# Eight-head projections, spread by DMA, and a re-timed feed-forward in a fused attention and SwiGLU kernel

## The chip, the core and the metric

The kernel runs on one core of one Trainium2 chip. The metric is the device time in microseconds (us) of one execution, as the median of several runs. A core has five engines that work side by side and wait for each other through semaphores: TensorE (PE, matmuls into PSUM, its weight loads shown as PEld), VectorE (DVE), ScalarE (ACT), GpSimd (POOL) and SyncE (SP), which here issues every DMA, in order, on one queue.

## What is computed

```python
def reference(A_x, A_wqkv, A_wo, B_x, B_w1, B_w3, B_w2):
    x = A_x                                   # [1, 2048, 512], bf16
    xn = _layernorm(x, axis=-1)
    return x + _A_ref(xn, A_wqkv, A_wo) + _B_ref(xn, B_w1, B_w3, B_w2)

# _A_ref: 32 heads of 16 columns
qkv = (x @ wqkv).reshape(B, S, 3, H, Dh).transpose(2, 0, 3, 1, 4)
scores = einsum("bhqd,bhkd->bhqk", q, k) * (Dh ** -0.5)
o = einsum("bhqk,bhkd->bhqd", softmax(scores), v)
out = o.transpose(0, 2, 1, 3).reshape(B, S, D) @ wo

# _B_ref: F = 1792
h = silu(x @ w1) * (x @ w3)
out = h @ w2
```

`B_x` is not read: both branches take the normalised `A_x`.

## The kernel before

**A planner writes the order.** The Python code does not loop over the chip's work directly. It holds queues of candidate steps (score blocks, exps, copies, matmul tiles, DMAs) with an estimated cost for each, repeatedly emits the one that could start first, and records every dependence as a semaphore wait. So each engine receives a fixed list of instructions, whose order follows from the cost estimates, and a change of one step can move all the others.

**Groups and units.** The 32 heads form 8 groups of 4, since one head has 16 columns and a group's four heads sit in four 32-row bands of the array. The 2048 query rows form 4 quarters of 512. A quarter and a group make a query group, 32 in all, worked in order. Each is cut into units of 256 query rows (the first into 128, 128, 256, the last into 256, 128, 128): 66 units.

**Two passes over the scores.** For every unit the scores are made twice. Pass 1 (`p1_cand`, matmuls at line 799) writes two heads' scores of 128 queries by 512 keys into two PSUM banks, and VectorE reduces them to a row maximum (line 821): 1024 reduces of 1024 columns. There are 16 of them in a unit of 256 queries; the count up to now is what the planner calls a step (`p1_n`). After a unit's last reduce its negated maximum (line 862) is split into two bf16 parts by GpSimd (lines 838 and 840), transposed by a DMA (line 859) and put by two DMAs (line 855) into rows 16 and 17 of each head's band of `QT`. Pass 2 (`p2_cand`, line 935) makes the scores again, transposed, with these two rows adding minus the maximum, and ScalarE's exp (line 948) writes the probabilities into a slot of `PT` (44 slots of 512 columns, the first 16 of which hold x during the layer norm). A unit of 256 queries takes 32 exps, one of 128 takes 16. For the first two and the last three units (`FAST_AUG`) the two rows come from a matmul instead (`tile_QT2`), which projects the unit's queries again and adds the shift.

**After the exps.** `tile_PV` multiplies the probabilities with `Vaug`, the values with a column of ones; it may begin when at most 4 of the unit's exps are left (`PV_LEFT`), and gives its `PT` slots back as it goes. The sums of the exps are inverted and spread by a chain of transfers and GpSimd operations (lines 1031 to 1057, one unit at a time), except in the last three units (`FAST_PV`), where a second set of matmuls with ones and VectorE's reciprocal (line 1001) and product (line 1003) do it.

**Projections.** A key tile (`tile_KT`) is one group's keys for 512 rows: 16 matmuls and a copy by ScalarE (line 560) that adds a one to rows 16 and 17 through `kbias`. A query tile (`tile_QT`) is the same for a query group (copy at line 603). Their weights are kept in a padded form, 32 columns for a head, 16 of them zero. `QT` has three slots; slot ug % 3 can be written again when pass 2 has issued all matmuls of query group ug - 3.

**Feed-forward.** 14 blocks of 128 columns for each quarter, 56 steps. Each is a gate and an up tile of 16 matmuls, three ScalarE copies (lines 665, 667, 671) and three GpSimd operations (lines 650 to 654) into `hT`, which holds one quarter. `ffn_from` gives the step of pass 1 from which each may start. `tile_OUT` adds x, the feed-forward product and the projected attention of 128 rows; in the last quarter `tile_OUTA` does all but the attention and `tile_OUTB` the rest.

**Order of the column tiles.** `choose` hands out one tile at a time while pass 1 runs: a projection with a due step less than 8 ahead first, then PV, a projection less than 20 ahead, outputs, feed-forward, a projection less than 80 ahead. `fill_cand` adds matmuls without use where TensorE's load is low.

Of the kernel before, what the change touches and what calls it, by code (L numbers as in the profile page):

```python
# [5 lines left out]
FP32 = mybir.dt.float32  # L6
# [229 lines left out]
def _build(nc, A_x, A_wqkv, A_wo, B_w1, B_w3, B_w2, out):  # L236
# [12 lines left out]
    NPT = 44  # L249
# [8 lines left out]
    LAG = 44  # L258
# [7 lines left out]
    for qc in range(NQC):  # L266
        for g in range(NG):
            last = qc == NQC - 1 and g == NG - 1
            first = qc == 0 and g == 0
            for (q0, nq) in ([(0, 256), (256, 128), (384, 128)] if last else  # L270
                             [(0, 128), (128, 128), (256, 256)] if first else [(0, 256), (256, 256)]):
                units.append((qc, g, q0, nq))
    NU = len(units)
    FAST_AUG = {0, 1, NU - 3, NU - 2, NU - 1}
    FAST_PV = {NU - 3, NU - 2, NU - 1}
# [7 lines left out]
    with ctx:  # L283
        PT = sb("PT", [128, NPT, 512], BF16)
        x_sb = PT[:, 0:NT, :]
        xr = sb("xr", [128, 4, D], BF16)
# [10 lines left out]
        hT = sb("hT", [128, FC, 512], BF16)  # L297
        stg = {"wk": 0, "wv": DC, "wq": 2 * DC}
        STG_KEYS = {w: [("hT", i) for i in range(o, o + DC)] for w, o in stg.items()}
        wkst, wv, wqst = (hT[:, stg[w]:stg[w] + DC, :] for w in ("wk", "wv", "wq"))  # L300
        kbias = sb("kbias", [128, 1], FP32)
        wq = sb("wq", [128, DC * NG * 4, 32], BF16)
        wk_on = sb("wk_on", [128, DC * NG * 128], BF16)
        on_b = sb("on_b", [128, NG, 512], BF16)
        wk = wk_on[:, :].rearrange("p (a b) -> p a b", b=32)
# [23 lines left out]
        maskrow = sb("maskrow", [1, 128], BF16)  # L329
        onesrow = sb("onesrow", [1, 2], BF16)  # L330
# [21 lines left out]
        def qt_keys(qs, q0, nq, what):  # L352
            return [(what, qs, q) for q in range(q0 // 128, (q0 + nq) // 128)]

# [23 lines left out]
        def c_small(e):  # L378
            e.memset(maskrow[:, :], 0.0)
            e.memset(onesrow[:, :], 1.0)  # L380
            e.memset(mhalf[:, :], -0.5)
            e.memset(mone[:, :], -1.0)
            return e.memset(Z[:, :, :, :], 0.0)
        P.op("pool", c_small, writes=[("maskrow",), ("onesrow",), ("mhalf",), ("mone",), ("Z", 0), ("Z", 1)], occ=1.2)
        P.op("pool", lambda e: e.memset(maskrow[0:1, :].rearrange("p (j d) -> p j d", d=32)[:, :, 16:18], 1.0),
             writes=[("maskrow",)], occ=0.1)
        P.op("dve", lambda e: e.memset(wk[:, :, 16:32], 0.0), writes=[("wkpad",)] + ON0_KEYS, occ=0.95)
        P.op("dve", lambda e: e.memset(wq[:, :, 16:32], 0.0), writes=[("wqpad",)], occ=0.95)
# [3 lines left out]
        P.op("pe", lambda e: e.matmul(bank(4)[:, 0:1], maskrow[0:1, :], onesrow[0:1, 0:1], start=True, stop=True),  # L392
             reads=[("maskrow",), ("onesrow",)], writes=[("ps", 4)], occ=0.05, lat=0.3)
# [13 lines left out]
        def load_w(dst, w, off):  # L407
            P.dma(lambda e: e.dma_start(dst, wqkv_v[:, :, off * D:(off + 1) * D]), writes=STG_KEYS[w], lat=5.0)
        load_x(0)
        load_x(1)  # L410
        load_w(wkst, "wk", 1)
        load_w(wqst, "wq", 0)
        load_x(2)
        load_x(3)
        load_w(wv, "wv", 2)
# [10 lines left out]
        def pad_first(dst, src):  # L426
            return lambda e: e.tensor_scalar(
                dst.rearrange("p (c h) d -> p c h d", c=DC)[:, :, 0:4, 0:16],
                src[:, :, 0:64].rearrange("p c (h d) -> p c h d", d=16), 1.0, 0.0, ALU.mult, ALU.add)

        def pad_rest(dst, src, c):
            return lambda e: e.tensor_scalar(
                dst[:, c * NG * 4 + 4:(c + 1) * NG * 4, 0:16],
                src[:, c, 64:D].rearrange("p (a d) -> p a d", d=16), 1.0, 0.0, ALU.mult, ALU.add)

        def pad_first_a(dst, src):
            return lambda e: e.activation(
                dst.rearrange("p (c h) d -> p c h d", c=DC)[:, :, 0:4, 0:16],
                src[:, :, 0:64].rearrange("p c (h d) -> p c h d", d=16), ACTF.Identity)

        def pad_rest_a(dst, src, c):
            return lambda e: e.activation(
                dst[:, c * NG * 4 + 4:(c + 1) * NG * 4, 0:16],
                src[:, c, 64:D].rearrange("p (a d) -> p a d", d=16), ACTF.Identity)
        wq_all = wq[:, :, :]
        poolq["pad"].append(_Item(pad_first(wk, wkst), STG_KEYS["wk"], [("wk", 0)], 0.4))
        miscq.append(_Item(pad_first_a(wq_all, wqst), STG_KEYS["wq"], [("wq", 0)], 0.3))
        for c in range(DC):
            poolq["pad"].append(_Item(pad_rest(wk, wkst, c), STG_KEYS["wk"], [("wk", 1 + c)], 0.62,
                                      pred=lambda: ("KT", 0, NQC - 1) in done))  # L450
        WK_KEYS = [("wkpad",)] + [("wk", i) for i in range(DC + 1)] + ON0_KEYS
        WQ_KEYS = [("wqpad",)] + [("wq", i) for i in range(DC + 1)]
        wq4 = wq[:, :, :].rearrange("p (c g j) d -> p c g (j d)", c=DC, g=NG)
        wk4 = wk.rearrange("p (c g j) d -> p c g (j d)", c=DC, g=NG)
        poolq["pad"].append(_Item(lambda e: e.memset(Vaug[:, :, :, 16:17], 1.0), [],
                                  [("Vone",)], 2.4, pred=lambda: ("AUG", 0) in done))
        poolq["pad"].append(_Item(lambda e: e.memset(wo[:, :, :], 0.0), [], [("wo",)], 3.5,
# [62 lines left out]
        def tr_ready(t):  # L520
            done.add(("xn", t))
            pt_free.append(t)
            head_tiles.append(tile_tr(t))
            if t % XG == XG - 1:
                gi = t // XG
                head_tiles.append(tile_KT(0, gi))
                if gi == 0:
                    head_tiles.append(tile_QT(0))
# [22 lines left out]
        def tile_KT(g, sc, need=None):  # L551
            groups = []
            for c in range(DC):
                groups.append((lambda bk, c=c: col_groups(
                    bk, lambda i: wk4[:, c, g, 32 * i:32 * i + 32], lambda i: xnT[:, c, sc * 512:(sc + 1) * 512], 512,
                    start=c == 0, stop=c == DC - 1),
                    (WK_KEYS if g else [("wkpad",), ("wk", 0)]) + xnT_keys(sc * 512, 512), _c_mm(512), None))

            def evac(bk):
                return [_Item(lambda e: e.activation(KT[:, g, sc * 512:(sc + 1) * 512], bank(bk), ACTF.Identity,  # L560
                                                     bias=kbias[:, 0:1]),
                              [("ps", bk), ("kbias",)], [("KT", g, sc)], 0.57, 0.68,
                              cb=lambda op: done.add(("KT", g, sc)), name="first")]
            return _Tile("KT%d_%d" % (g, sc), groups, evac, need=need,
                         pred=lambda: all(("xnT", t) in done for t in range(sc * 4, sc * 4 + 4))
                         and (g == 0 or not poolq["pad"] or not _wk_pending()))

        def _wk_pending():
            return any(it.writes and it.writes[0][0] == "wk" for it in poolq["pad"])

        def tile_V(t, need=None):
            groups = []
            for c in range(DC):
                groups.append((lambda bk, c=c: col_groups(
                    bk, lambda i: xnT[:, c, t * 128 + 32 * i:t * 128 + 32 * i + 32], lambda i: wv[:, c, :], D,
                    start=c == 0, stop=c == DC - 1), STG_KEYS["wv"] + [("xnT", t)], _c_mm(512), None))
# [11 lines left out]
        def qt_groups(qc, g, q0, nq, stop_last):  # L588
            groups = []
            for c in range(DC):  # L590
                groups.append((lambda bk, c=c: col_groups(
                    bk, lambda i: wq4[:, c, g, 32 * i:32 * i + 32],
                    lambda i: xnT[:, c, qc * 512 + q0:qc * 512 + q0 + nq], nq,
                    start=c == 0, stop=stop_last and c == DC - 1, skip=not stop_last),
                    (WQ_KEYS if g or qc else [("wqpad",), ("wq", 0)]) + xnT_keys(qc * 512 + q0, nq), _c_mm(nq), None))
            return groups

        def tile_QT(ug, need=None):
            qc, g = divmod(ug, NG)
            qs = ug % 3  # L600

            def evac(bk):
                return [_Item(lambda e: e.activation(QT[:, qs, :], bank(bk), ACTF.Identity),  # L603
                              [("ps", bk)], qt_keys(qs, 0, 512, "QT"), _c_act(512),
                              cb=lambda op: done.add(("QT", ug)))]
            return _Tile("QT%d" % ug, qt_groups(qc, g, 0, 512, True), evac, need=need,
                         pred=lambda: (ug < 3 or p2_units_done[0] > ug_last[ug - 3])
                         and all(("xnT", t) in done for t in range(qc * 4, qc * 4 + 4))
                         and (ug == 0 or not _wq_pending()))

        def _wq_pending():
            return any(it.writes and it.writes[0][0] == "wq" for it in miscq)

        def tile_QT2(u):
# [10 lines left out]
            def evac(bk):  # L625
                return [_Item(lambda e: e.activation(QT[:, qs, q0:q0 + nq], bank(bk)[:, 0:nq], ACTF.Identity),
                              [("ps", bk)], qt_keys(qs, q0, nq, "QT"), _c_act(nq), cb=lambda op: done.add(("AUG", u)))]
# [5 lines left out]
        def ffn_from(sc, fc):  # L633
            last = sc == NQC - 1
            lo = sc * CHUNK + (100 if sc else 40)
            hi = (sc + 1) * CHUNK + (-48 if last else LAG)
# [801 lines left out]
```

## Time and profile before

| | us |
|---|---|
| median of 3 runs (1233.07 to 1240.68) | 1234.11 |
| the profiled execution | 1235.43 |
| its span, first to last instruction | 1233.4 |
| mean granted TensorE clock | 0.998 |

| group of instructions | count | busy us |
|---|---|---|
| pass 2 scores, matmul, L935 | 4224 | 568.3 |
| pass 1 scores, matmul, L799 | 2048 | 441.9 |
| key copies, ACT, L560 | 32 | 23.2 |
| query copies, ACT, L603 | 32 | 20.3 |
| gate and up copies, ACT, L665, L667, L671 | 168 | 105.6 |
| filler and x, matmul, `xnT` by `ident` | 1412 | 111.7 |

The profile gives the busy time of each engine, the chain of work that ended last, groups of instructions by line, a timeline, and busy times in chosen windows. In a group's line the columns are line, engine, operation, output and input tiles, count, then busy time, mean ns of one, and the idle time ahead of them with what ended it. Instructions of one engine overlap a little, so the mean of one can be longer than its share of the busy time. In a row of windows with all engines the order is PE, PEld, DVE, ACT and POOL, each with its number of instructions, then the granted TensorE clock, the DMA share and GB/s; a row for one line has the one engine.

### The profile page before, as it was taken

What the parts mean: (1) busy time and instruction counts of PE and PEld (TensorE: products, weight loads), DVE (VectorE), ACT (ScalarE), POOL (GpSimd) and SP (SyncE); (2) the same over time, 40 slices, a digit from 0 to 9 for tenths busy, and PEclk for the clock granted to TensorE, in tenths of its full rate; (3) what the DMA queues carried; (4) which work ended last, traced back from release to release, by engine and by line L of the source; (5) the groups of instructions that cost most, each with busy time, mean ns of one, the idle gap of its engine ahead of it and who ended that gap; (6) DMA issues with size and microseconds to landing.
All of it is one profiled execution on the core that took longest, in us unless ns stands there. A gap on an engine that the chain in (4) does not pass through costs nothing.

```text
span 1233.4 us, 39009 instructions
## 1 busy us (share of the span) xinstructions
PE 1164.6 (94%) x16813; PEld 449.9 (36%) x16813; DVE 1196.3 (97%) x1150; ACT 1181.3 (96%) x2407; POOL 357.6 (29%) x453
## 2 busy tenths in 40 slices
PE   5999999999999999999999999999999999999997
PEld 2433333333333333333333333333333333333344
DVE  8999999999999999999999999999999999999982
ACT  5899999999999999999999899999999999999997
POOL 3214222233221114333322113332432113545110
PEclk9999999999999999999999999999999999999999
DMA  7101101011001012111110111111110102111000
GB/s 213 21 19 29 23 18 28 17 26 20 17 18 28 16 29 44 20 24 28 28 25 19 26 26 29 37 20 24 28 28 16 27 17 52 41 37 20 9 7 21
DMA packets 113236, 36.24 MB, mean 29 GB/s; under 512 B 98560, under 2 KB 113064, under 8 KB 113064
## 3 DMA queue, kind: packets, MB, share of 16 engines
q1 hardware_dynamic: 113064, 33.76, 12.8%
q8 instruction: 131, 2.15, 0.7%
q14 instruction: 41, 0.34, 0.1%
HBM read 22.81 MB, written 2.10 MB: 20 GB/s over the span
## 4 chain that ended last, share of the span: by engine, by line
ACT 68%; PE 20%; DVE 6%; DMA 4%; issue 1%; POOL 1%; SPq 1%; ACTq 0%; POOLq 0%
ACT PT L948 58%; PE ps L471 11%; PE ps L935 5%; DVE part L821 5%; PE ps L799 3%; ACT th L665 2%; ACT zg L667 2%; ACT ub L671 2%; DMA Zs<-Z 2%; ACT KT L560 1%; ACT QT L603 1%; ACT U L1012 1%; DMA QT<-Zs 1%; ACT xnT L544 1%; DMA hT<-in_A_wqkv_dram 0%
## 5 line engine op out<-in xcount | busy, mean ns | idle before, releaser
L821 DVE TENSOR_REDUCE part<-ps 128x2 f32<-128x1024 f32 x1024 | 1169.8, 1215 | 6.6 <-PE ps L799 3.4
L948 ACT ACTIVATE PT<-ps 128x512 bf16<-128x512 f32 x2048 | 1050.0, 640 | 19.6 <-PE ps L935 18.1
L935 PE MATMUL ps<-QT,KT 32*128 32x256 bf16 (+1 forms) x4224 | 568.3, 269 | 12.8 <-DMA QT<-Zs 2.9
L799 PE MATMUL ps<-KT,QT 32*128 32x512 bf16 x2048 | 441.9, 383 | 3.1 <-DVE part L821 2.7
L935 PEld LDWEIGHTS ps<-QT,KT 32*128 32x128 bf16 x4224 | 203.3, 92 | 300.5 <-ACT PT L948 129.2
L1035 POOL TENSOR_TENSOR Rc<-Lc,mone 128x8 f32<-128x8 f32 (+1 forms) x63 | 101.9, 1618 | 388.7 <-DMA Lc<-U 388.7
L471 PE MATMUL ps<-PT,Vaug 128*17 128x256 bf16 (+1 forms) x4224 | 179.6, 271 | 4.0 <-ACT PT L948 1.2
L471 PE MATMUL ps<-xnT,w 128*32 128x512 bf16 x1792 | 148.0, 386 | 20.2 <-ACT zg L667 14.9
L799 PEld LDWEIGHTS ps<-KT,QT 32*128 32x128 bf16 x2048 | 115.5, 91 | 112.9 <-issue 60.2
L471 PEld LDWEIGHTS ps<-PT,Vaug 128*17 128x17 bf16 x4224 | 84.6, 89 | 91.9 <-issue 68.6
L471 PE MATMUL ps<-xnT,ident 128*32 128x512 bf16 x1412 | 111.7, 384 | 6.8 <-DVE osb L753 0.2
L652 POOL TENSOR_TENSOR a<-zg,ub 128x512 f32<-128x512 bf16 x56 | 64.7, 1155 | 69.8 <-ACT ub L671 69.8
L471 PE MATMUL ps<-w,hT 128*32 128x512 bf16 x896 | 79.5, 386 | 0.0
L838 POOL TENSOR_SCALAR Z<-negm 128x8 bf16<-128x8 f32 (+1 forms) x65 | 14.9, 229 | 212.3 <-DVE negm L862 212.0
L471 PEld LDWEIGHTS ps<-xnT,w 128*32 128x32 bf16 x1792 | 38.5, 94 | 92.6 <-issue 79.4
L654 POOL TENSOR_TENSOR hT<-a,t 128x512 bf16<-128x512 f32 x56 | 71.1, 1269 | 3.4
L471 PEld LDWEIGHTS ps<-xnT,ident 128*32 128x32 bf16 x1412 | 27.6, 94 | 55.6 <-ACT PT L948 41.3
L471 PE MATMUL ps<-xnT,wq 128*32 128x512 bf16 (+2 forms) x592 | 44.5, 371 | 1.8 <-ACT zg L667 0.3
L650 POOL TENSOR_SCALAR t<-th 128x512 f32<-128x512 bf16 x56 | 34.9, 623 | 37.0 <-ACT th L665 36.1
L471 PE MATMUL ps<-xnT,wk_on 128*32 128x512 bf16 x512 | 41.1, 392 | 3.6 <-ACT xnT L544 1.7
L1057 POOL TENSOR_TENSOR on_b<-U,R 128x256 bf16<-128x256 f32 (+1 forms) x33 | 23.5, 712 | 65.5 <-DMA R<-Rrow 65.5
L1057 POOL TENSOR_TENSOR wk_on<-U,R 128x256 bf16<-128x256 f32 x30 | 21.9, 728 | 58.0 <-DMA R<-Rrow 58.0
(75 smaller groups left out, 429.6 us busy)
## 6 DMA issues: line engine op xcount, KB each, us to landing
w<-in_B_w_dram SPq DMA_DIRECT2D x112, 128.0 KB
R<-Rrow SPq DMA_DIRECT2D x244, 16.0 KB
PT<-in_A_x_dram SPq DMA_DIRECT2D x4, 512.0 KB
xr<-in_A_x_dram SPq DMA_DIRECT2D x16, 128.0 KB
out_dram<-osb SPq DMA_DIRECT2D x16, 128.0 KB
QT<-Zs SPq DMA_DIRECT2D x122, 2.0 KB
w<-in_B_w_dram SPq DMA_DIRECT2D x1, 1792.0 KB
hT<-in_A_wqkv_dram SPq DMA_DIRECT2D x3, 512.0 KB
```

Source lines behind the costliest of these rows:

```text
L471: ins = e.matmul(bank(bk)[32 * i:32 * i + m, c0:c0 + ncols], make_lhsT(i), rhs_ap(i), start=start, stop=stop, tile_position=(0, 32 * i), **kw)
L650: q.append(_Item(lambda e: e.tensor_scalar(t1[:, :], th[:, ss, :], 1.0, 1.0, ALU.mult, ALU.add), [("th", ss)], [("t1",)], 0.62, 0.72))
L652: q.append(_Item(lambda e: e.tensor_tensor(a32[:, :], zg[:, ss, :], ub[:, ss, :], ALU.mult), [("zg", ss), ("ub", ss)], [("a32",)], 1.1, 1.25))
L654: q.append(_Item(lambda e: e.tensor_tensor(hT[:, fc, :], a32[:, :], t1[:, :], ALU.mult), [("a32",), ("t1",)], [("hT", fc)], 1.25, 1.35, cb ...
L665: return [_Item(lambda e: e.activation(th[:, ss, :], bank(bk), ACTF.Tanh, scale=0.5), [("ps", bk)], [("th", ss)], _c_act(512), cb=part_don ...
L667: _Item(lambda e: e.activation(zg[:, ss, :], bank(bk), ACTF.Identity, scale=0.5), [("ps", bk)], [("zg", ss)], _c_act(512), cb=part_done, n ...
L799: ins = e.matmul(bank(2 * sl + i), QT[32 * j:32 * j + 32, qs, q * 128:(q + 1) * 128], KT[32 * j:32 * j + 32, g, kc * 512:(kc + 1) * 512], ...
L821: redq.append(_Item(lambda e: e.tensor_reduce(part[:, par, qt, 2 * pair:2 * pair + 2, kc], ps[:, sl * 1024:(sl + 1) * 1024].rearrange("p ( ...
L935: ins = e.matmul(bank(b)[:, i * nq:(i + 1) * nq], KT[32 * j:32 * j + 32, g, (k0 + i) * 128:(k0 + i + 1) * 128], QT[32 * j:32 * j + 32, qs, ...
L948: expq.append(_Item(lambda e: e.activation(PT[:, sl, :], bank(b), ACTF.Exp, scale=SCALE), [("ps", b)], [("PT", sl)], _c_act(512), cb=cb))
L1035: poolq["nrm"].append(_Item(lambda e: e.tensor_tensor(Rc[:, pp, 0:nl], Lc[:, pp, 0:nl], mone[:, 0:nl], ALU.pow), [("Lc", pp), ("mone",)], ...
L1057: poolq["nrm"].append(_Item(lambda e: e.tensor_tensor(onorm[ob][:, g, q0:q0 + nq], U[:, us, 0:nq], R[:, pp, 0:nq], ALU.mult), [("U", us)] ...
```

## The change

- **Projections of up to eight heads.** `tile_heads` takes the weights as they are in memory (16 columns a head, no zero columns), projects two groups at once into one bank, and copies it by one ScalarE operation into one of two buffers `kq`. DMAs then spread it: 4 for each group, 16 rows each, into the 32-row bands of `KT` or `QT`. From query group 3 on, two more DMAs set rows 16 and 17 of the `QT` slot back to zero, from zero rows of `wo`. Only group 0's first tiles and the last group's augmented queries keep padded weights.
- **Constant rows.** The ones in rows 16 to 31 of `KT` and the zeros of `QT` are written by fills, group 1 by VectorE, the others by GpSimd.
- **Feed-forward.** `hT` has 28 slots instead of 14, and the 56 steps are due evenly between steps 40 and 660 of pass 1.
- **Memory.** `PT` has 34 slots instead of 44, `xr` 2 instead of 4.
- **Units.** The last three query groups are cut into units of 128; the last four units take their shift rows by matmul, the last three the fast normaliser. There are 71 units.

```diff
-    NPT = 44
+    NPT = 34
+    ONES_PAIR = 1.0 + 2.0 ** -9 - 2.0 ** -16
+    NKQ = 2
...
-    LAG = 44
+    NHT = 28
+    UNIT_HEAD = (128, 128, 256)
+    UNIT_TAIL = {1: (128, 128, 128, 128), 2: (128, 128, 128, 128), 3: (128, 128, 128, 128)}
+    NFAST = 4
+    NFPV = 3
+    NXR = 2
+    FFN_LO = 40
+    FFN_HI = 660
+    LEAD_Q = 8
+    LEAD_K = 6
+    HEAD_Q = 16
+    HEAD_K = 16
...
+        P.op("dve", lambda e: e.memset(padded, 0.0), writes=[("wk0",), ("wq0",)] + ON0_KEYS, occ=0.6)
+        P.op("dve", lambda e: e.memset(wq_last[:, :, :], 0.0), writes=[("wq7",)], occ=0.4)
+        P.op("dve", lambda e: e.memset(QT[:, :, :], 0.0),
...
+        def ones_rows(g):
+            return (lambda e: e.memset(KT[:, g, :].bitcast(FP32), ONES_PAIR)), [k for sc in range(NQC)
+                                                                              for k in kh_keys(g, sc)]
+        for g in range(1, 5):
+            f, keys = ones_rows(g)
+            P.op("dve" if g == 1 else "pool", f, writes=keys, occ=1.1)
...
+        def tile_heads(what, g0, ng, sc, need):
+            w = wk if what == "K" else wq
...
+                        for i in range(2 * ng):
+                            ins = e.matmul(bank(bk)[32 * i:32 * i + 32, :],
+                                           w[:, c, 64 * g0 + 32 * i:64 * g0 + 32 * i + 32],
+                                           xnT[:, c, sc * 512:(sc + 1) * 512], start=c == 0, stop=c == DC - 1,
+                                           tile_position=(0, 32 * i))
...
+                    again = what == "Q" and ug >= 3
...
+                    for r in range(2 if again else 0):
+                        left[0] += 1
+                        later_dma(lambda e, r=r, qs=qs: e.dma_start(QT[16 + r:128:32, qs, :], wo[16:128:32, 0, :]),
+                                  [("wo",)], qt_keys(qs, 0, 512, "QTr%d" % r), cb=cb,
+                                  pred=lambda ug=ug: p2_units_done[0] > ug_last[ug - 3])
+                    for j in range(4):
+                        src = kq[64 * h + 16 * j:64 * h + 16 * j + 16, b, :]
+                        if what == "K":
+                            later_dma(lambda e, j=j, g=g, src=src: e.dma_start(
+                                KT[32 * j:32 * j + 16, g, sc * 512:(sc + 1) * 512], src),
+                                [("kq", b)], kh_keys(g, sc, (j,)), cb=cb)
+                        else:
+                            later_dma(lambda e, j=j, qs=qs, src=src: e.dma_start(QT[32 * j:32 * j + 16, qs, :], src),
+                                      [("kq", b)], qh_keys(qs, 0, 512, (j,)), cb=cb,
+                                      pred=lambda ug=ug: ug < 3 or p2_units_done[0] > ug_last[ug - 3])
+
+            def evac(bk):
+                b = box[0]
+                return [_Item(lambda e: e.activation(kq[0:rows, b, :], bank(bk)[0:rows, :], ACTF.Identity),
+                              [("ps", bk)], [("kq", b)], _c_act(512), cb=spread)]
...
         def ffn_from(sc, fc):
-            last = sc == NQC - 1
-            lo = sc * CHUNK + (100 if sc else 40)
-            hi = (sc + 1) * CHUNK + (-48 if last else LAG)
-            return lo + (hi - lo) * fc // FC
+            return FFN_LO + (FFN_HI - FFN_LO) * (sc * FC + fc) // (NQC * FC)
...
-                return all(("OUT", (sc - 1) * 4 + ts) in done for ts in range(4))
+                return idx < NHT or all(("OUT", (idx - NHT) // FC * 4 + ts) in done for ts in range(4))
...
-        for ug in range(1, NQC * NG):
-            crit.append(tile_QT(ug, need=32 * ug if ug > 1 else 20))
-        for g in range(1, NG):
+        for qc in range(NQC):
+            for g0 in range(0 if qc else 1, NG, 2):
+                crit.append(tile_heads("Q", g0, min(2, NG - g0) if not qc or g0 else 2, qc,
+                                       need=32 * (qc * NG + g0) - LEAD_Q if qc or g0 > 1 else HEAD_Q))
+        for g0 in range(1, NG, 2):
             for sc in range(NQC):
-                crit.append(tile_KT(g, sc, need=32 * g + 4 * sc if g > 1 else 21 + 4 * sc))
+                crit.append(tile_heads("K", g0, min(2, NG - g0), sc,
+                                       need=32 * g0 + 4 * sc - LEAD_K if g0 > 1 else HEAD_K + 4 * sc))
```

## The prediction

> **What bounds the kernel now.** I read first the page's engine totals, the chain of waits and the costliest groups.
>
> ```profile
> PE 1164.6 (94%) x16813; PEld 449.9 (36%) x16813; DVE 1196.3 (97%) x1150; ACT 1181.3 (96%) x2407; POOL 357.6 (29%) x453
> ...
> ACT 68%; PE 20%; DVE 6%; DMA 4%; issue 1%; POOL 1%; SPq 1%; ACTq 0%; POOLq 0%
> ...
> L821 DVE TENSOR_REDUCE part<-ps 128x2 f32<-128x1024 f32 x1024 | 1169.8, 1215 | 6.6 <-PE ps L799 3.4
> L948 ACT ACTIVATE PT<-ps 128x512 bf16<-128x512 f32 x2048 | 1050.0, 640 | 19.6 <-PE ps L935 18.1
> ```
>
> VectorE has 1024 reduces (1169.8/1024 = 1.142 us each), which no part of the change touches. ScalarE has two exps behind each reduce, 0.49 us from start to start (runs such as 24 in 11.76 us), so 0.98 of every 1.142 us before its other work. Then the timelines of VectorE and of ScalarE at the end:
>
> ```profile
> 1190.15 8.14 DVE L821 TENSOR_REDUCE part<-ps 128x2 f32<-128x1024 f32 x7
> 1198.32 0.17 DVE L862 TENSOR_REDUCE negm<-part 128x4 f32<-128x16 f32 x1
> ...
> 1228.72 0.96 DVE L1001 RECIPROCAL R<-ps 128x128 f32<-128x128 f32 x1 [5.61 <-PE ps L471]
> 1229.71 0.29 DVE L1003 TENSOR_TENSOR wk_on<-ps,R 128x128 bf16<-128x128 f32 x1
> 1230.51 0.69 DVE L753 TENSOR_TENSOR osb<-ps,zg 128x512 bf16<-128x512 f32 x1 [0.51 <-PE ps L471]
> ```
> ```profile
> 1200.23 0.28 ACT L626 ACTIVATE QT<-ps 128x128 bf16<-128x128 f32 x1
> ...
> 1218.32 9.67 ACT L948 ACTIVATE PT<-ps 128x512 bf16<-128x512 f32 x19 [0.36 <-PE ps L935]
> ```
>
> The last reduce ends at 1198.3; 35.1 us follow, in which ScalarE still runs 53 exps. Only 16 of them belong to the last unit; 37 (18 us) are backlog. Where it comes from, the windows show: the gate activations of the feed-forward part (L665), then all engines.
>
> ```profile
> 780.00:1000.00 220.00, 6.12 (x10) 1.00 0.12 24
> 1000.00:1198.30 198.30, 8.61 (x14) 1.00 0.13 27
> ```
> ```profile
> 300.00:780.00 480.00, 461.92 (x6426) 174.14 (x6422) 477.91 (x445) 466.55 (x956) 136.62 (x169) 1.00 0.12 26
> 1000.00:1198.30 198.30, 189.65 (x2732) 73.20 (x2736) 196.55 (x184) 193.87 (x400) 70.34 (x84) 1.00 0.13 27
> 1198.30:1233.40 35.10, 27.05 (x736) 14.80 (x728) 7.88 (x13) 27.86 (x56) 2.37 (x2) 0.98 0.07 20
> ```
>
> A quarter of the 56 feed-forward steps (three ScalarE copies each) falls into the last 198 us, while ScalarE idles 13.5 us in 300 to 780 (fourth busy figure). From the times left in both streams: at 950 us 214 reduces and 478 exps are left, so exps are 49 behind (two per reduce), about the floor of one 32-exp unit plus the 7.2 us from a unit's maximum to its shift rows (996.44 to 1003.68). So the time is the last reduce plus a tail made of ScalarE's backlog.
>
> **The change, part by part.** The sum is made against the profiled run, 1235.43 us (span 1233.4, 2.03 around it); that is 1.3 above the median.
>
> *Projections.* Key tiles go from 28 to 16 beside group 0's, query tiles from 31 to 16. That is 27 ScalarE copies less at 0.49 (13 us) and 27 times four column groups less at 0.22 (24 us of TensorE). Both lie beside the reduces, so neither counts by itself; it is room.
>
> *Their price is on the SP queue:* 112 key, 124 query and 58 zero-row transfers, 294 issues of about 0.55 us (the row that writes QT from Zs has a median of 551 ns) = 162 us more on a queue that issues some 700 now. Queued behind a spread of eight (4.4 us) stand the shift rows and the normaliser's transfers. A shift row late by 4.4 us delays ScalarE only when it has caught up, and it then has room; key tiles are asked for 6 steps ahead of use and chosen at least 8 before that (14 x 1.142 = 16 us) against 4.4 of issue, about 2 to land, and 2 to 4 of matmuls and copy. I count 0; uncovered it is some 5 us for a group.
>
> *Feed-forward earlier.* All 56 steps are due by step 660 instead of 976. Up to there (41 units of 16 reduces, 18.28 + 0.09 us each) ScalarE must do per unit 32 exps (15.68), U (0.28), 168/41 copies (2.0) and 51/41 copies of projections, values and outputs (0.6): 18.6 against 18.37. Exps fall 0.23 x 41 = 9.4 us (19 exps) further behind, to 68. After 660 a unit costs 15.68 + 0.28 + 0.12 (queries) + 0.17 (outputs) = 16.25, so 2.1 us are won in each of 22.75 units: 48 us, five times what is needed. The 37 exps of backlog are gone by the end. Limit: queries hold three slots, so the exps can be at most 128 behind, less about 10 for 5.5 us of refilling a slot by DMA: 118, far from 68.
>
> *34 probability slots for 44.* Ten slots are 4.9 us of cover for ScalarE; the matmuls that free slots start only when 28 of a unit's 32 exps are out, so 4 + 2 exps (2.9 us) cover them where it was 7.8. Before shows ScalarE waiting 18.1 us for L935 in the whole run. I take 0.2 us a unit (bounds 0 and 1.5; a feed-forward tile ahead in the bank takes about 4 us). This goes off the room above: 0 in the sum.
>
> *VectorE.* Zero fills go from 4096 bf16 columns (2 x 0.91) to 1024 + 512 + 1536, and ones for group 1 take another 2048: 2.28 against 1.82, two more gaps of 0.1, less the 0.49 that it idles for x: +0.2. Five more units, 0.09 each for the maximum (958.22 to 958.31): +0.45. The third-last unit's reciprocal and product (0.96 + 0.29) fall ahead of the last reduce: +1.25 (0 to 2.5). GpSimd's three fills of 2048 columns (at most 1.76 us each by the 0.86 ns of an element in its fill of wo) start at 2.2 and end before the weights that it waits for until 7.8: 0.
>
> *TensorE's clock* is a fresh cost, since less real work is left in the last third. One place shows it:
>
> ```profile
> 594.00:596.00 2.00, 2.00 (x20) 0.44 (x12) 1.30 (x2) 1.37 (x4) 0.00 (x0) 0.51 0.17 34
> ```
>
> The granted clock falls to 0.51 and VectorE loses 0.70 us, after ten microseconds in which TensorE was over 85% busy, with filler matmuls among it. I add one such event: +0.7 (0 to 15, rival 3). The Trainium skill (TensorE: Matmul & The Clock Gate, "What's actually happening") has the array throttled to half rate only after an idle window of about 3.4 us. By that rule the sum holds 0 here instead of 0.7; the half rate agrees with the trace, the idle window does not.
>
> *The tail.* With the backlog gone: last reduce to the end of the copy of the augmented query 2.2 (1198.3 to 1200.51), 0.5 to the first exp, 16 exps 7.85, and from the last exp's end (1227.99) to the end of the span 5.4: 16.0. TensorE has 32 output groups (6.9 us) to fit in; between 1198.8 and 1205.6 it did 24 beside the exps at 0.5 us of ScalarE idle, so +1 (0 to 4.5 if they queue). Tail 17.0 instead of 35.1. The 128-wide units put 16 instead of 32 exps in each of the last steps and cost TensorE nothing that shows: two exps take 0.41 us of its time at 128 columns and 0.39 at 256.
>
> Sum: last reduce 1198.3 + 0.2 + 0.45 + 1.25 + 0.7 = 1200.9; span 1217.9; with 2.03, 1219.9; less 1.3, **1218.6**.
>
> **Rivals.**
> 1. *The 34 slots starve ScalarE a little.* Let b be its loss in each unit. Backlog at 660 is 9.4 + 41b us and is worked off at 2.1 - b a unit: both this and the 118-exp limit are used up at b = 0.6. Beyond it VectorE stalls 41(b - 0.6) and the tail keeps 22.75(b - 0.6): 63.75 us for each us. At b = 0.75 the time is 1228. For: cover falls from 7.8 to 2.9 us and a tile in the way takes 4. Against: projections no longer compete, and such a tile is in the way in some units alone.
> 2. *Slower: the same wait taken whole.* From b = 0.85 nothing is gained, from 1.04 it is over 1% slower; b = 1.2 gives 1218.6 + 38 = 1257. Place: ScalarE waiting for L935 at each unit's change before step 660, then VectorE waiting for L799 at each group's start because the query slot is still held. For: between 100 and 350 us ScalarE shows no idle time at all. Against: every unit would have to lose more than its own cover of 2.9 us misses on average.
> 3. *The clock.* If the drop comes once a unit in the last 22 units, 22 x 0.7 = 15 us: 1234. Against: one event in 1233 us, and the filler stays.
> 4. *The feed-forward does not get early.* Step 42 must wait until the second quarter's outputs are out (about step 590, where 505 is due); were the rest to drag past 900 by slow outputs, the backlog would stay: 1232. Against: 14 steps need about 14 x 4 us, so they end near step 650.
>
> **How the numbers follow.** Forecast 0.68, rivals 0.10, 0.14, 0.04, 0.04. A measurement here tells about 1% (12.3 us) from no change: bounds 1221.8 and 1246.5. Of the forecast's own range, 1212 to 1224 (VectorE's 6 us of inner idle gone at the lower end; +4.5 of queued groups at the upper), 0.62 lies below 1221.8, 0.06 above. Within 1%: 0.06 + 0.10 + 0.04 + 0.04 = 0.24; slower 0.14. The range goes up to 1236 to take in rivals 1, 3 and 4; outside are rival 2 and a few hundredths below.
>
> **What will show it.** Right: last reduce near 1201 and 16 to 20 exps after it; no L665 activation later than about 800 us; exps under 100 behind at 750 us. Wrong: VectorE idle over 10 us between 60 and 1190, released by the matmuls of line 799 (rival 2); ScalarE's wait for the score matmuls far above 18 us with the backlog kept (rival 1); a granted clock under 0.95 in several windows after 800 (rival 3).

## The result, and the profile after

The changed kernel takes 1220.83 us (median of 4 executions, 1220.60 to 1221.68) against 1234.72 us before (the same three runs as in the table above and one more); the ratio is 0.988, with a 95% interval of 0.985 to 0.991. The forecast was 1218.6.

The page of the changed kernel (line 902 is now the reduce, 1029 the exp, 1016 pass 2's matmuls; the columns are as before):

```profile
PE 1155.5 (95%) x17141; PEld 461.3 (38%) x17141; DVE 1195.6 (98%) x1157; ACT 1162.6 (95%) x2382; POOL 366.7 (30%) x476
...
ACT 52%; PE 33%; DVE 10%; issue 2%; DMA 1%; SPq 1%; POOL 0%; ACTq 0%
...
L902 DVE TENSOR_REDUCE part<-ps 128x2 f32<-128x1024 f32 x1024 | 1169.9, 1215 | 6.6 <-PE ps L1016 3.2
L1029 ACT ACTIVATE PT<-ps 128x512 bf16<-128x512 f32 x2048 | 1043.4, 643 | 13.8 <-PE ps L1016 12.8
```

VectorE's work is what it was; ScalarE has 18.7 us less. What is new shows at the end, first in VectorE's timeline, then in ScalarE's:

```profile
1190.78 8.02 DVE L902 TENSOR_REDUCE part<-ps 128x2 f32<-128x1024 f32 x7
1198.84 0.17 DVE L943 TENSOR_REDUCE negm<-part 128x4 f32<-128x16 f32 x1
...
1214.29 0.96 DVE L1083 RECIPROCAL R<-ps 128x128 f32<-128x128 f32 x1 [0.19 <-PE ps L494]
...
1216.08 0.69 DVE L833 TENSOR_TENSOR osb<-ps,zg 128x512 bf16<-128x512 f32 x1 [0.51 <-PE ps L494]
```
```profile
1199.41 2.28 ACT L1029 ACTIVATE PT<-ps 128x512 bf16<-128x512 f32 x4 [0.48 <-PE ps L1016]
1201.59 0.27 ACT L703 ACTIVATE QT<-ps 128x128 bf16<-128x128 f32 x1
1201.75 3.90 ACT L1029 ACTIVATE PT<-ps 128x512 bf16<-128x512 f32 x7
1206.53 2.68 ACT L1029 ACTIVATE PT<-ps 128x512 bf16<-128x512 f32 x5 [0.88 <-PE ps L1016]
1209.51 1.57 ACT L1029 ACTIVATE PT<-ps 128x512 bf16<-128x512 f32 x3 [0.31 <-PE ps L1016]
1211.27 2.17 ACT L1029 ACTIVATE PT<-ps 128x512 bf16<-128x512 f32 x4 [0.18 <-PE ps L1016]
```

The last reduce ends at 1198.8 instead of 1198.3, so nothing was won there. After it come 23 exps instead of 53, and the tail is 20.2 us instead of 35.1. All of the gain is tail. The windows show why: the gate activations, by stretch (now line 739).

```profile
780.00:1000.00 220.00, 4.47 (x7) 1.00 0.10 21
1000.00:1198.30 198.30, 0.00 (x0) 1.00 0.08 15
```

Before, these two stretches had 10 and 14 of them. How far the exps are behind two per reduce follows from what is left of both lines, reduces first and exps second:

```profile
600.00:1219.00 619.00, 597.93 (x524) 1.00 0.10 21
1150.00:1219.00 69.00, 48.80 (x43) 1.00 0.07 16
```
```profile
600.00:1219.00 619.00, 567.09 (x1125) 1.00 0.10 21
1150.00:1219.00 69.00, 60.34 (x119) 1.00 0.07 16
```

At 600 us 1125 exps and 524 reduces are left, so the exps are 1125 - 2 x 524 = 77 behind (before 49); in the same way 75 at 850 (47), 46 at 1050 (49) and 33 at 1150 (60). ScalarE falls behind in the middle and has caught up at the end. The prediction and the expectations work with busy times divided by the mean of one instead of with these counts; that gives up to 11 less (66 at 600 us in the changed kernel), since exps overlap more in some stretches than in others.

### The profile page after: what moved, and what is told of

It reads as the page before. It is cut to its first block, busy times and chain, and to the rows that moved or that the text cites. A ratio compares the mean times of both kernels' runs of the same rounds, so it can differ in the third digit from the quotient of the medians.

```text
span 1219.0 us, 40324 instructions
## 1 busy us (share of the span) xinstructions
PE 1155.5 (95%) x17141; PEld 461.3 (38%) x17141; DVE 1195.6 (98%) x1157; ACT 1162.6 (95%) x2382; POOL 366.7 (30%) x476
## 4 chain that ended last, share of the span: by engine, by line
ACT 52%; PE 33%; DVE 10%; issue 2%; DMA 1%; SPq 1%; POOL 0%; ACTq 0%
ACT PT L1029 45%; PE ps L494 17%; DVE part L902 10%; PE ps L1016 9%; PE ps L880 5%; ACT th L739 2%; ACT zg L741 2%; PE ps L602 1%; ACT kq L649 1%; ACT ub L745 1%; SPq L639 1%; ACT U L1093 1%; DMA KT<-kq 1%; ACT xnT L567 1%; DMA wk_on<-in_A_wqkv_dram 0%
## 5 line engine op out<-in xcount | busy, mean ns | idle before, releaser
L902 DVE TENSOR_REDUCE part<-ps 128x2 f32<-128x1024 f32 x1024 | 1169.9, 1215 | 6.6 <-PE ps L1016 3.2
L1029 ACT ACTIVATE PT<-ps 128x512 bf16<-128x512 f32 x2048 | 1043.4, 643 | 13.8 <-PE ps L1016 12.8
L1016 PE MATMUL ps<-QT,KT 32*128 32x256 bf16 (+1 forms) x4544 | 577.7, 262 | 10.4 <-DMA QT<-Zs 1.9
L880 PE MATMUL ps<-KT,QT 32*128 32x512 bf16 x2048 | 435.8, 384 | 4.4 <-DVE part L902 4.0
L1016 PEld LDWEIGHTS ps<-QT,KT 32*128 32x128 bf16 x4544 | 219.8, 92 | 291.6 <-ACT PT L1029 131.9
L494 PE MATMUL ps<-PT,Vaug 128*17 128x256 bf16 (+1 forms) x4544 | 185.9, 265 | 6.2 <-ACT zg L741 2.3
L880 PEld LDWEIGHTS ps<-KT,QT 32*128 32x128 bf16 x2048 | 112.5, 91 | 115.9 <-issue 54.4
L494 PE MATMUL ps<-xnT,ident 128*32 128x512 bf16 x1556 | 123.0, 384 | 7.2 <-ACT kq L649 0.4
L1141 POOL TENSOR_TENSOR wk_on<-U,R 128x256 bf16<-128x256 f32 (+1 forms) x35 | 23.1, 660 | 88.1 <-DMA R<-Rrow 88.1
L724 POOL TENSOR_SCALAR t<-th 128x512 f32<-128x512 bf16 x56 | 34.8, 621 | 13.7 <-ACT th L739 11.8
L745 ACT ACTIVATE ub<-ps 128x512 bf16<-128x512 f32 x56 | 35.3, 631 | 0.0
L741 ACT ACTIVATE zg<-ps 128x512 bf16<-128x512 f32 x56 | 35.2, 628 | 0.0
```

The source lines that it names most:

```text
L494: ins = e.matmul(bank(bk)[32 * i:32 * i + m, c0:c0 + ncols], make_lhsT(i), rhs_ap(i), start=start, stop=stop, tile_position=(0, 32 * i), **kw)
L724: q.append(_Item(lambda e: e.tensor_scalar(t1[:, :], th[:, ss, :], 1.0, 1.0, ALU.mult, ALU.add), [("th", ss)], [("t1",)], 0.62, 0.72))
L741: _Item(lambda e: e.activation(zg[:, ss, :], bank(bk), ACTF.Identity, scale=0.5), [("ps", bk)], [("zg", ss)], _c_act(512), cb=part_done, n ...
L745: return [_Item(lambda e: e.activation(ub[:, ss, :], bank(bk), ACTF.Identity), [("ps", bk)], [("ub", ss)], _c_act(512), cb=part_done)]
L880: ins = e.matmul(bank(2 * sl + i), QT[32 * j:32 * j + 32, qs, q * 128:(q + 1) * 128], KT[32 * j:32 * j + 32, g, kc * 512:(kc + 1) * 512], ...
L902: redq.append(_Item(lambda e: e.tensor_reduce(part[:, par, qt, 2 * pair:2 * pair + 2, kc], ps[:, sl * 1024:(sl + 1) * 1024].rearrange("p ( ...
```

## Experiments

The TensorE clock that is granted differs between executions of one and the same kernel, and the time with it: 47 executions of the kernel before fit 0.8 us for each 0.001 of mean clock (1.000: 1234.7; 0.983: 1247.4). The table therefore gives, beside the comparison with the kernel before on the same chip, the shortest execution with its own clock. Two kernels are best compared where these clocks are alike.

| kernel | ratio to before, 95% interval | shortest, us (clock) |
|---|---|---|
| before | | 1233.2 (0.999) |
| changed, first measurement | 0.988, 0.985 to 0.991 | 1220.6 (0.997) |
| changed, beside the experiments | 0.991, 0.987 to 0.994 | 1221.1 (0.996) |
| 1 late feed-forward | 1.004, 1.001 to 1.007 | 1236.3 (0.998) |
| 2 one group at a time | 0.999, 0.996 to 1.003 | 1228.5 (0.999) |
| 3 one small group | 0.996, 0.994 to 0.999 | 1224.9 (0.998) |
| 4 before, small last units | 1.005, 1.000 to 1.009 | 1243.6 (0.989) |
| 6 more filler | 1.001, 0.999 to 1.004 | 1230.9 (0.985) |
| 7 no filler | 1.066, 1.057 to 1.076 | 1309.4 (0.832) |
| 8 slots 30 | 0.996, 0.993 to 0.998 | 1225.1 (0.997) |
| 9 shift rows first | 1.071, 1.068 to 1.074 | 1322.2 (0.975) |
| 10 feed-forward from 110 | 1.003, 0.999 to 1.006 | 1232.5 (0.988) |
| 11 exps first in the tail | 0.994, 0.991 to 0.996 | 1225.1 (0.993) |
| 12 three buffers | 1.012, 1.009 to 1.015 | 1245.0 (0.984) |

### Which part brings the gain: 1 to 4

**1. Late feed-forward.**

```diff
-            return FFN_LO + (FFN_HI - FFN_LO) * (sc * FC + fc) // (NQC * FC)
+            last = sc == NQC - 1
+            lo = sc * CHUNK + (100 if sc else 40)
+            hi = (sc + 1) * CHUNK + (-48 if last else 44)
+            return lo + (hi - lo) * fc // FC
```

> The changed kernel with the due steps of the feed-forward as before the change (quarter by quarter, the last one between steps 868 and 976), all else as changed. Theory A (the gain is ScalarE's backlog, removed by the earlier feed-forward): the last reduce stays near 1199 us, 40 or more exps follow it, and the time is 1233 to 1238 us. Theory B (the gain is the 27 ScalarE copies that the shared projections save): 1221 to 1225. Theory C (the gain is the small last units): 1221 to 1225.

At a clock of 0.998 it takes 1236.3 us: the whole gain is gone. In its profile (an execution at 0.995) 14 gate activations lie between 1000 us and the last reduce (1201.3), and this is the stretch behind it in the windows of all engines, beside the same row of the changed kernel (second fence; it begins half a microsecond ahead of the end of the last reduce):

```profile
1201.30:1234.90 33.60, 28.05 (x868) 16.41 (x866) 7.00 (x14) 26.40 (x52) 3.38 (x5) 0.98 0.08 22
```
```profile
1198.30:1219.00 20.70, 15.98 (x496) 9.19 (x488) 7.44 (x14) 13.08 (x26) 1.88 (x3) 1.00 0.10 30
```

52 ScalarE instructions in 33.6 us, 26 in 20.7: 47 exps follow the last reduce instead of 23, the backlog is back. Theory A holds: without the earlier feed-forward neither the saved copies nor the small units bring anything. No run has the earlier feed-forward alone.

**2. One group at a time.**

```diff
-            for g0 in range(0 if qc else 1, NG, 2):
-                crit.append(tile_heads("Q", g0, min(2, NG - g0) if not qc or g0 else 2, qc,
+            for g0 in range(0 if qc else 1, NG):
+                crit.append(tile_heads("Q", g0, 1, qc,
...
-        for g0 in range(1, NG, 2):
+        for g0 in range(1, NG):
             for sc in range(NQC):
-                crit.append(tile_heads("K", g0, min(2, NG - g0), sc,
+                crit.append(tile_heads("K", g0, 1, sc,
```

> The changed kernel with projections of one group at a time: the spreading transfers stay as many, the copies go back from 32 to 59 outside group 0 (27 x 0.49 = 13 us of ScalarE). Theory A: that goes off the room that ScalarE has in the last third, 1219 to 1224 us. Theory B: 1232 to 1236. Theory C: 1219 to 1224.

1228.5 at 0.999 is between the two theories, some 8 us more than the changed kernel. It is not the copies alone that come back: the projections' copies take 35.8 us of ScalarE instead of 20.0, and their matmuls, which now fill two of the four bands, 77.3 us of TensorE instead of 42.2. The run does not tell the two apart. Its profile is of an execution at a mean clock of 0.970 (1251.5 us), with half rate from 92 to 106 us and again from 1154, so only its course in between is used. The exps are 106 behind at 600 us and 98 at 850, where the changed kernel has 77 and 75, and still 66 at 1150. The feed-forward ends at 880 us instead of 832, and ScalarE, though far behind, stands in order on copies of output tiles, four times between 950 and 1030, 6.9 us in all, such as:

```profile
1008.02 0.60 ACT L804 ACTIVATE osb<-ps 128x512 bf16<-128x512 f32 x1 [2.38 <-PE ps L494]
```

So what the shared projections save is not all spare room: the earlier feed-forward is in part paid with it. Theory A alone falls.

**3. One small group** (`UNIT_TAIL = {1: (128, 128, 128, 128)}`).

> The changed kernel with units of 128 queries in the last query group alone instead of the last three. Theory A: ScalarE has caught up either way, so within 3 us of the changed kernel, 1219 to 1224. Theory C: a good part of the gain goes, 1226 to 1234.

1224.9 at 0.998 is 4 us more than the changed kernel at 0.997. Its other executions lie from 1226.6 to 1237.1 at clocks of 0.997 down to 0.988. At like clocks it is 4 to 6 us slower (1229.3 and 1230.9 at 0.993, where the changed kernel has 1225.1), and in its profile 39 exps follow the last reduce instead of 23, in a tail of 27.0 us instead of 20.2. So theory A's "caught up either way" does not hold, and the small units of the other two groups are worth some 4 to 6 of the 14 us, between the two theories.

**4. The kernel before with small last units.** Its fast units share the buffer of reciprocals with the normal ones, so some rows are scaled by another unit's sums: it leaves out the half of that buffer which the changed kernel keeps for them.

```diff
-            last = qc == NQC - 1 and g == NG - 1
+            last = qc == NQC - 1 and g >= NG - 3
...
-            for (q0, nq) in ([(0, 256), (256, 128), (384, 128)] if last else
+            for (q0, nq) in ([(0, 128), (128, 128), (256, 128), (384, 128)] if last else
...
-    FAST_AUG = {0, 1, NU - 3, NU - 2, NU - 1}
+    FAST_AUG = {0, 1, NU - 4, NU - 3, NU - 2, NU - 1}
```

> The kernel before with units of 128 queries in its last three query groups and its last four units taking the shift rows by matmul; feed-forward and projections as before. Theory A: the backlog stays, over 45 exps follow the last reduce, 1231 to 1237 us. Theory C: 1220 to 1226.

No gain by itself: at 0.989 it takes 1243.6 and 1244.4, where 0.8 us for each 0.001 puts the kernel before at about 1242. Theory A's 1231 to 1237 is missed too, with the clock. Most of its executions had a clock of 0.949 to 0.966 and took 1263 to 1278; the profile is of one of these, with 50 exps after the last reduce, and shows the reason, which belongs to the next part.

### The clock: 5 to 7

**5. The changed kernel again.**

> The changed kernel as it is, beside the others on the same chip: 1219 to 1224 us at a granted clock of 0.994 or more. If the clock of single executions differs, the time should follow it by about 0.9 us for each 0.001 of mean clock, as in the executions of the late feed-forward (0.998: 1236, 0.979: 1254).

1221.1 at 0.996 to 1229.5 at 0.990: 1.3 us for each 0.001, steeper than expected. At 0.994 or more there are 1221.1, 1222.9 and 1224.6, the last just outside the range.

**6 and 7. More filler** (`LOAD_MIN = 15000`) **and none** (`LOAD_MIN = 0`).

> The changed kernel with the planner's load floor at 15000 columns in 2.3 us instead of 12500, so more filler matmuls. Theory D (the clock falls when too few columns stream, as in the stretches with a load under 0.4): no window between 60 and 1190 us under a clock of 0.95, VectorE's idle time between 80 and 140 us under 2 us instead of about 5, and 1215 to 1219 us. Theory E (the filler's own matmuls are what is in the way there): VectorE's idle time grows and the time is 1222 to 1235.

> The changed kernel without filler matmuls. Theory D: long stretches at a clock of 0.5, mean clock under 0.97, time over 1240 us. Theory F (the clock falls only after TensorE idles for some 3.4 us, which it never does here): the clock stays above 0.99 and the time within 1217 to 1223.

Without filler the mean clock is 0.80 to 0.83 and the time over 1300 us, although TensorE is busy for 95% of the span and, from 30 us to the last reduce, never idle for more than 1.8 us at a time. One of the long stretches:

```profile
1190.00:1300.00 110.00, 109.20 (x1643) 69.67 (x1640) 97.29 (x93) 96.52 (x198) 17.59 (x38) 0.50 0.06 9
```

Theory F falls, and theory D's times come as forecast: taking the filler out brings the clock down. For what it goes by I work out, from the matmuls in the timeline, the share of columns that the four bands could stream. Where the clock holds, this share is mostly 0.41 to 0.6. It is 0.38 in the two microseconds ahead of the drop in the changed kernel, 0.30 ahead of that of the kernel before. That is not a threshold: about 40 of the 561 two-microsecond stretches of the changed kernel between 60 and 1190 us in which the clock held have a share under 0.38 too. How low it must be, and for how long, was not found. A drop near the end can last to the last reduce, perhaps because at half rate the same work streams fewer columns in a microsecond. The windows of experiment 4 (third-last figure: clock):

```profile
1100.00:1150.00 50.00, 46.62 (x762) 22.89 (x760) 48.12 (x48) 48.79 (x101) 20.43 (x29) 0.93 0.11 21
1150.00:1225.00 75.00, 75.00 (x998) 37.83 (x994) 52.60 (x49) 56.50 (x107) 13.17 (x25) 0.50 0.04 6
```

For 75 us the clock is 0.50, TensorE is busy throughout, and VectorE works 52.6 of the 75. But more filler did not help: experiment 6 has no execution over 0.985, and its clock falls at 129 us, at 170 and at 1181. At each of the three TensorE was standing in order on something late, where filler behind it cannot run: 1.98 us up to 130.3 on a shift row, 1.05 us up to 170.4 on a copy that waited for a buffer of projected heads, and at the end again on a shift row:

```profile
1180.99 0.63 PE L1016 MATMUL ps<-QT,KT 32*128 32x128 bf16 x12 [2.04 <-DMA QT<-Zs]
```

So D's remedy failed. Theory E's time came at best (1230.9), but at these three places late transfers, and not the filler, were in the way.

### Slots, the SP queue and the tail: 8 to 12

**8. 30 slots** (`NPT = 30`).

> The changed kernel with 30 probability slots instead of 34, four exps (2 us) less cover for ScalarE at each change of unit. Theory G (the slots already bind, as rival 1 had it): exps over 90 behind at 600 us and 1228 us or more. Theory H (34 have room left): exps under 75 behind at 600 us and 1219 to 1224 us.

By count the exps are 90 behind at 600 us, by busy times, as the bounds were set, 81 (the changed kernel 77 and 66); the shortest execution takes 1225.1 at 0.997: between the theories. Four slots less let ScalarE fall 13 exps further behind. What that costs is open: 4 us more than the changed kernel at 0.997, by one execution, but 1229.8 and 1230.6 at 0.990, where that has 1229.5.

**9. Shift rows first.** The transfers that spread keys and queries carry the name.

```diff
-                    s = cand("sp", it, True)
+                    s = cand("sp", it, True) + (3.0 if it.name == "spread" else 0.0)
```

> The changed kernel with one difference in the planner's choice for the SP queue: a spreading transfer counts as ready 3 us later than it is, so that a unit's transposition, shift rows and normaliser transfers that come up within 3 us go ahead of it. Theory S (VectorE's lost 5 us between 80 and 140 come from shift rows late behind bursts of eight spreads; the matmuls of pass 2 then hold up pass 1 in TensorE's queue and the load dips): VectorE's idle time there under 2 us, no clock under 0.9 there, 1214 to 1219 us at a mean clock of 0.997. Theory P (the place is simply too full of projections and feed-forward): idle time and time as in the changed kernel, 1219 to 1224.

A clear miss: 1322 us. VectorE's timeline between 40 and 320 us has waits such as these:

```profile
99.27 1.23 DVE L902 TENSOR_REDUCE part<-ps 128x2 f32<-128x1024 f32 x1 [23.93 <-PE ps L880]
...
185.94 4.62 DVE L902 TENSOR_REDUCE part<-ps 128x2 f32<-128x1024 f32 x4 [15.94 <-PE ps L880]
```

They stand on pass 1 (line 880), which waits for `KT<-kq` (up to 11 us in TensorE's own list). Between 70 and 96.7 us SP issues only three key transfers. The normaliser's transfers go ahead of the others, and SP, which works in order, stands on them until their data is there: by its timeline it is busy only 59% of the time between 60 and 270 us. Theory S is not refuted by this, but the remedy puts the keys behind transfers that are not ready: there is little slack for either.

**10. Feed-forward from step 110** (`FFN_LO = 110`).

> The changed kernel with the feed-forward due from step 110 instead of 40 (the end stays at 660). Theory P: VectorE's idle time between 80 and 140 us falls under 2 us, 1215 to 1219 us. Theory S: it stays or grows, since ScalarE is caught up and every late shift row shows; 1220 to 1228, also because more of the feed-forward is left for later.

VectorE's idle time between 80 and 140 us is 3.2 us, where the two profiles of the changed kernel have 4.4 and 4.8, so neither forecast of it holds; between 100 and 200 us it is 5.8 (3.3 and 5.9). The exps are 90 behind at 850 us instead of 75. Theory P's time is far off, so the place is not simply too full of feed-forward. All ten executions have a clock of 0.988 or less, and 1232.5 at 0.988 is about what 1.3 us for each 0.001 makes of the changed kernel's 1229.5 at 0.990. So the later start goes with a lower clock; what it costs beside that is not shown.

**11. Exps first in the tail** (`TAIL_LOW = 1`).

> The changed kernel with TAIL_LOW 1 instead of 0: after the last reduce TensorE serves pass 2 as soon as at most one exp is queued, ahead of the output groups. If ScalarE's gaps in the tail (0.48, 0.88, 0.31 and 0.18 us in the changed kernel) are on the path, the tail after the last reduce falls from 20.2 to 18 to 19 us; if the output groups are only pushed behind the last exp, it stays within 0.7 us of 20.2.

Neither: the tail is 23.6 us. ScalarE's gaps do shrink, but only 3 output groups (of four matmuls) now run between 1204 and 1216 us, where the changed kernel has 19, and the clock is 0.55 between 1210 and 1215 us. By the shortest execution it is no better than the changed kernel at that clock (1225.1 at 0.993 both).

**12. Three buffers** (`NKQ = 3`, `NPT = 33`).

> The changed kernel with three buffers for projected heads instead of two, paid for with one probability slot (33). Theory Q (the two buffers bind the keys' path in the first 300 us, as the kernel with late spreads suggests): VectorE's idle time between 20 and 200 us falls from 7 to under 4 us, 1216 to 1220 us at a mean clock of 0.997. Theory R (the SP queue's order binds, not the buffers): idle time there 5 us or more, and 1220 to 1225 at that clock.

Theory Q falls: VectorE's idle time does not shrink (8.5 us between 20 and 200), and the time is 1245 or more, which theory R's 1220 to 1225 misses too. Around 130 us its profile shows theory R's case bare. SP's timeline, then TensorE's and VectorE's:

```profile
124.27 1.24 SPq L940 DMA_TRANSPOSE Zs<-Z  x1
...
126.21 3.93 SPq L639 DMA_DIRECT2D KT<-kq  x5
...
133.83 1.85 SPq L639 DMA_DIRECT2D KT<-kq  x3
...
136.97 1.16 SPq L936 DMA_DIRECT2D QT<-Zs  x2
```
```profile
139.47 0.62 PE L1016 MATMUL ps<-QT,KT 32*128 32x256 bf16 x8 [3.60 <-DMA QT<-Zs]
```
```profile
141.93 1.23 DVE L902 TENSOR_REDUCE part<-ps 128x2 f32<-128x1024 f32 x1 [4.24 <-PE ps L1016]
```

A unit's maximum is sent to be transposed at 124.3; its shift rows are issued at 137.0, since eight key transfers and nine others are ahead of them in the queue. TensorE stops in order at pass 2, pass 1 behind it cannot run, VectorE idles 4.2 us, and the clock falls. After this the exps are 78 behind at 200 us and stay 15 to 32 behind the changed kernel's course. How much of the 24 us is due to that and how much to the 33 slots and the clock stays open.

From the timelines, SP is busy 81% of the time between 60 and 270 us in the changed kernel, 41% before. No version tried beats the changed kernel.

## Why the prediction was right, step by step

- **The tail is ScalarE's backlog: right.** Experiment 1 puts the backlog and the whole loss back. The tail is 20.2 us against 17.0 forecast, with 23 exps against the 16 to 20 named. Of the 3.2 us, 0.8 is the copy of the augmented query (its end is at 1201.9, 3.0 after the last reduce instead of 2.2: four output groups ran ahead of it), and 1.5 are three exps of the unit before, still to run behind it. The other 0.9 is mostly ScalarE waiting for score matmuls between the exps. The small units, whose 16 exps the sum counted in, are part of this: by experiment 3 those of two groups are worth 4 to 6 us.
- **Last reduce at 1200.9: 1198.8, with its terms off in both directions.** The zero fills cost 0.1 (the layer norm starts at 4.81 against 4.72) where 0.2 was put. Nothing stands between the last reduces of the third-last unit and the last: the fast normaliser came after them, so its 1.25 were not paid. In gaps of over 0.15 us VectorE has 6.8 us of idle time up to 200 us (before 1.5) and almost none later (before 4.0); with the small gaps it is 8.3 us instead of 7.6 between the first and the last reduce. That the total is only 2.2 us off is in part luck: 2.1 too much up to the last reduce stands against 3.2 too little behind it, and the 1.3 taken off for the median is not there, since the changed kernel's median is that of its profiled run within 0.1.
- **Feed-forward done by step 660: it ended later,** with the last gate activation at 832 us (step 703). Between 600 and 700 us there is none. This is rival 4's wait for the outputs of the second quarter; it was harmless, because 370 us remained.
- **"Neither counts by itself; it is room": wrong by 8 us.** This is the step that failed. The sum held 48 us of room after step 660 and let what the shared projections save (13 us of copies and 24 of TensorE; measured by experiment 2, 16 and 35) go off it. Experiment 2 takes that back and loses 8, although only 13 of the 48 us were to go. The rate of 2.1 us a unit is seen for a while: from 850 to 950 us the changed kernel wins back 24 exps, 11.8 us in 5.5 units. But the feed-forward is done only at 832, and from 950 on, with the exps 51 behind, ScalarE waits for work again. In experiment 2, with more to win back, it does not hold: from 850 to 1150 us 32 exps, about 1 us a unit. The sum let ScalarE run without a stop there, and 6.9 us of waits for output tiles, the later end of the feed-forward and the extra copies stand in its way. How much of the 8 us is due to each stays open.
- **Spread transfers at 0, "uncovered some 5 us": the cover is thin.** The profiled run loses 5 us of VectorE's time before 200 us, against the kernel before, 2.4 of them in the eight microseconds around its drop of the clock (below). Experiments 9 and 12 show both ways in which the queue fails.
- **34 slots: 0 is not contradicted for 34:** ScalarE waits 12.8 us for the score matmuls in the whole run, 18.1 before. With four fewer it falls further behind (experiment 8), so what rivals 1 and 2 rest on is seen; their slope is not measured.
- **The clock at 0.7 us: mis-sized.** The profiled run has one drop, but a long one:

```profile
128.00:134.00 6.00, 6.00 (x70) 1.81 (x74) 4.51 (x4) 4.17 (x9) 2.56 (x3) 0.50 0.11 21
```

Six microseconds at half rate cost VectorE 1.5 us in them (4.51 of 6.00), and the next two another 0.9. Rival 3's price holds for a short drop alone; one that begins near 1150 us can last until the reduces are done, as experiment 4 shows. What the Trainium skill (TensorE: Matmul & The Clock Gate, "What's actually happening") says of the half rate is seen in every such row. Its idle window is not: experiment 7 is at half rate for long stretches with TensorE 95% busy, and in experiment 4 TensorE is not idle at all in the three microseconds ahead of the drop at 1143 us.

## What to carry to other kernels

Where one engine has a fixed stream and a second follows it, the end is set by how far the second is behind at the last item, so move its optional work to where it is least late, and count on the room only after subtracting everything that moves there and the waits in which the second engine stands in order. Work taken from two busy engines and put on an in-order DMA queue needs that queue's occupancy in the worst stretch, not its mean: 41% became 81% here, and a 4 us burst then stands ahead of a transfer that two engines wait for. A part of a change that brings nothing by itself (here the saved copies and the small units without the earlier feed-forward) can still be what pays for another.

## What the runs showed of the hardware that was not expected

- The granted clock did not follow whether TensorE is busy: the drops of the two kernels began after ten microseconds with TensorE 89% and 92% busy (65% and 90% in the last two), and one at 1143 us in experiment 4 held for 82 us with TensorE always busy. It went with how many columns stream (0.30 and 0.38 of what the bands could, in the two microseconds ahead of the two drops), but shares as low stand without a drop too.
- The mean clock of single executions of one kernel on one chip varied from 0.983 to 1.000 (the kernel before, 1247 to 1233 us), and in experiment 8 from 0.746 to 0.997. The time spreads with it, so the clock has to be read with every time.
